# Letting GpSimd's jobs wait for the vector engine's last listed job on the shared SBUF port

## The chip, the cores and the metric

The kernel runs on one core of a Trainium2 chip. A core has five engines that work side by side, each through its own list of instructions, in order: TensorE (PE in the profile, with its weight loads as PEld), VectorE (DVE), ScalarE (ACT), GpSimd (POOL) and SyncE (SP), which here starts the transfers between HBM and SBUF. An instruction starts when those in front of it on its engine have been started and the semaphores that it names have reached their values. The metric is the time of one execution on the device, in microseconds (us); less is better.

## The reference

Attention with normalised queries and keys, and then two feed-forward layers, all in float32:

```python
def _attn_ref(q, k, v, g_q, g_k):           # batch 4, 12 heads, 448 rows, 64 columns
    q_n, k_n = (rmsnorm(q, g_q), rmsnorm(k, g_k))
    scores = q_n @ k_n.T / sqrt(64);  scores -= max(scores)
    attn = exp(scores);  attn /= sum(attn) + 1e-9
    return attn @ v

x = attention output as 1792 tokens x 768
h = x @ w_in;  x = (max(h, 0) ** 2) @ w_out                   # inner width 2048
g = x @ w_gate;  out = (g * sigmoid(g) * (x @ w_val)) @ w_out  # inner width 1536
```

## The kernel before

**Precision and tiles.** Products are made of float32 numbers split into a high and a low part: `hi` is a rounded copy, `lo = x - hi`, and a product is three matmuls (hi hi, hi lo, lo hi). So nearly every operand costs a copy (ACT or DVE, line 218 or 220 when it goes through `copy`) and a subtraction (DVE or POOL). Weights come as 64-bit words and are taken apart on DVE: lines 282 to 297 make the value from the two halves, 312 its low part. The attention goes over 24 pairs of heads; a pair has seven tiles of 128 rows. For each pair the kernel loads k and q (`kq`), squares them (`nat`, line 501 on POOL or 500 on ACT), sums the rows on DVE (506), finds the reciprocal root by three Newton steps (`rsqrt`: on DVE as one job for the first rows, else a begin on DVE, lines 448 and 449, and three jobs on POOL, lines 454 to 465, the last of which writes `stage`), lets PE transpose the result (`rows<-ident,stage`, 612), scales k (680, 683, or 595), splits k and q (`kst`, `kst_lo`, `qst`, `qst_lo`, 667), and then makes scores on PE (739), maxima on DVE (767, 768), exponentials on ACT (781), transposes on PE (845), their copies (218), the product with v (878), its scaling (900), and the split of the result into `x` (924 on POOL). The first part of the first feed-forward layer (`h_a`, `ya`) fills PE's gaps.

**The order of the work** is found while the program is built. The kernel is written as many small threads that yield jobs. A job names for each engine that may do it a planned time in ns; a planner with a clock of its own hands out the jobs, and in the order in which it hands them out the instructions are put on the engines' lists. That order is the list of work. On the chip each engine goes through its own list; between engines only the semaphores of the data hold.

The planner has a notion of a port that DVE and POOL share. A job's key `"G"` is POOL; `"W"` is DVE with operands in SBUF; `"V"` is DVE with an operand in PSUM, or a small one. A job on POOL and a `"W"` job on DVE are "ported": the planner starts one only when the last one's planned time is over.

```python
engines = {"P": nc.tensor, "A": nc.scalar, "V": nc.vector, "G": nc.gpsimd, "S": nc.sync}
def ported(job, e):
    return e == "G" or e == "V" and "W" in job[1][0]
...
if port[0] > clock[0]:
    q = [job for job in q if not ported(job, e)]
...
for e in engines:                     # who is asked, and in which order
    moved = dispatch(e) or moved
...
yield {"G": 900}, lambda e: step(e, ends if i == 2 else [(y, None)])      # rsqrt, three times
yield {"G": 1106, "W": 535}, lambda e: e.tensor_tensor(out=lo, in0=x, in1=as_f32(hi), op=ALU.subtract)
```

The exclusion is in the plan alone: in the program of before no semaphore stands for the port.

Of the kernel before, what the change touches and what calls it, by code (L numbers as in the profile page):

```python
# [78 lines left out]
def attention_two_ffn_kernel(  # L79
# [19 lines left out]
    nc = tc.nc  # L99
# [32 lines left out]
    engines = {"P": nc.tensor, "A": nc.scalar, "V": nc.vector, "G": nc.gpsimd, "S": nc.sync}  # L132
# [37 lines left out]
                heapq.heappush(timers, (clock[0] + p, serial[0], t, None))  # L170
            return

    port = [0.0]

    def meant(job):
        e = next(iter(job[1][0]))
        return "V" if e == "W" else e

    def cost(job, e):
        costs = job[1][0]  # L180
        return costs["W"] if e == "V" and "W" in costs else costs[e]

    def ported(job, e):
        return e == "G" or e == "V" and "W" in job[1][0]

    def late(job):

        e = meant(job)
        ahead = [o for o in queues[e] if not o[3] and (o[0].rank, o[2]) < (job[0].rank, job[2]) and meant(o) == e]
        return max(free_at[e] - clock[0], 0) + sum(cost(o, e) for o in ahead) + cost(job, e)  # L190

    def dispatch(e):
        queues[e] = [job for job in queues[e] if not job[3]]
        if not queues[e] or free_at[e] > clock[0]:
            return False
        q = [job for job in queues[e] if e == meant(job) or late(job) > cost(job, e) + spare[e]]
        if port[0] > clock[0]:
            q = [job for job in q if not ported(job, e)]
        if not q:
            return False  # L200
        job = min(q, key=lambda job: (job[0].rank, job[2]))
        job[3] = True
        t, p, _, _ = job
        p[1](engines[e])
        done = free_at[e] = clock[0] + cost(job, e)
        if ported(job, e):
            port[0] = done
        if e == "S":
            dma_free[0] = max(dma_free[0], clock[0] + 1100) + p[2] / DMA_RATE
            done = dma_free[0] + 900  # L210
        else:
            done += p[2] if len(p) > 2 else settle[e]
        heapq.heappush(timers, (done, job[2], t, e))
        return True
# [13 lines left out]
    def simulate(done):  # L228

        while not done():  # L230
            moved = True
            while moved:
                moved = False
                for entry in sorted(blocked, key=lambda entry: (entry[0].rank, entry[0].n)):
                    if entry[1]():
                        blocked.remove(entry)
                        resume(entry[0], None)
                        moved = True
                for e in engines:
                    moved = dispatch(e) or moved  # L240
            if done():
                return
            times = [timers[0][0]] if timers else []
            times += [free_at[e] for e in engines if queues[e] and free_at[e] > clock[0]]
            times += [port[0]] * (port[0] > clock[0])
            clock[0] = min(times)
            while timers and timers[0][0] <= clock[0]:
                _, _, t, value = heapq.heappop(timers)
                resume(t, value)
# [1063 lines left out]
```

## Time and profile before

| | |
|---|---|
| time of three runs | 1293.56, 1297.56, 1297.2 us; median 1297.2 |
| the profiled execution | 1290.19 us; its span, first to last instruction, 1288.4 us |
| busy in the span | PE 1258.1 us (98%), DVE 667.6 (52%), ACT 573.0 (44%), POOL 156.3 (12%) |
| granted TensorE clock | 0.999 of full speed in the mean |

The attention takes about the first 420 us; what follows is the two feed-forward layers. Names such as `kst_lo<-kq,kst` say what an instruction writes and reads. Busy PE time is modelled from pipelined matmuls.

### The profile page before, as it was taken

Reading aid. Unit: us, or ns where it says so; the run is one execution under the profiler, and the core shown is the slowest. Engines: PE = TensorE matmul, PEld = TensorE weight load, DVE = VectorE, ACT = ScalarE, POOL = GpSimd, SP = SyncE. Lnnn points to the kernel's source line nnn. Section 1 sums busy time; section 2 is a strip of 40 time slices with the busy share of each in tenths; the row PEclk is TensorE's granted clock in tenths of the full one; section 3 lists DMA queues with packets and bytes.
Section 4 is the critical chain, followed back from the end, with each engine's and each line's share of the span. In section 5 each row is a group of like instructions: output and inputs, shape, how many; then the busy total and the mean of one; then the engine's idle time right before and its main releaser. Section 6 shows DMA issues by size and latency. Waiting matters only on the chain.

```text
span 1288.4 us, 18441 instructions
## 1 busy us (share of the span) xinstructions
PE 1258.1 (98%) x6710; PEld 1079.9 (84%) x6710; DVE 667.6 (52%) x1357; ACT 573.0 (44%) x1257; POOL 156.3 (12%) x263
## 2 busy tenths in 40 slices
PE   8878999999999999999999999999999999999998
PEld 6555777777777999999999999999999999999998
DVE  7999964554543997249333783212148712213122
ACT  6898986776775656135322442212126411202110
POOL 4443633443210000000000000000000000000000
PEclk9999999999999999999999999999999999999999
DMA  6567564344313667137343563010127500203021
GB/s 210 150 200 197 161 189 124 110 123 134 93 43 104 209 192 254 52 114 226 113 129 129 172 206 126 21 65 7 37 63 232 154 1 1 86 1 129 1 86 43
DMA packets 85469, 151.02 MB, mean 117 GB/s; under 512 B 14641, under 2 KB 64962, under 8 KB 85378
## 3 DMA queue, kind: packets, MB, share of 16 engines
q1 hardware_dynamic: 85378, 149.84, 37.0%
q8 instruction: 53, 0.87, 0.3%
q14 instruction: 38, 0.31, 0.1%
HBM read 120.75 MB, written 29.04 MB: 116 GB/s over the span
## 4 chain that ended last, share of the span: by engine, by line
PE 83%; DVE 7%; ACT 4%; DMA 2%; issue 2%; POOL 1%; SPq 0%; DVEq 0%; ACTq 0%; POOLq 0%
PE y L325 27%; PE h_v L325 14%; PE h_g L325 14%; PE h L325 12%; PE ya L325 4%; PE o L878 3%; PE pt L845 3%; PE h_a L325 3%; PE sc L739 3%; DVE sc L767 2%; ACT ring L781 2%; ACT turned_p L218 1%; DVE ss L506 1%; DMA raw_out<-in_w_out_dram 1%; PE h_lead L325 1%
## 5 line engine op out<-in xcount | busy, mean ns | idle before, releaser
L325 PE MATMUL h_v<-x,hi_v 128*128 128x448 f32 x576 | 164.4, 366 | 0.0
L325 PE MATMUL h_g<-x,hi_g 128*128 128x448 f32 x576 | 164.3, 366 | 0.0
L325 PE MATMUL y<-s,hi_o 128*128 128x448 f32 x576 | 164.1, 366 | 0.0
L325 PE MATMUL y<-s,hi_out 128*128 128x448 f32 x552 | 157.2, 366 | 0.0
L325 PE MATMUL h<-x,hi_in 128*128 128x448 f32 x516 | 147.4, 367 | 0.0
L378 DVE TENSOR_TENSOR sig<-h_g,sig 128x448 f32<-128x448 f32 x48 | 29.9, 623 | 216.7 <-ACT sig L377 216.7
L781 ACT ACTIVATE ring<-sc,m,rms 128x448 f32<-128x448 f32 x168 | 124.0, 741 | 29.8 <-PE pt L845 20.2
L377 ACT ACTIVATE sig<-h_g 128x448 f32<-128x448 f32 x48 | 26.1, 544 | 219.3 <-PE h_g L325 219.2
L325 PEld LDWEIGHTS h_v<-x,hi_v 128*128 128x128 f32 x576 | 108.2, 188 | 9.3
L325 PEld LDWEIGHTS h_g<-x,hi_g 128*128 128x128 f32 x576 | 108.2, 188 | 9.2
L325 PEld LDWEIGHTS y<-s,hi_o 128*128 128x128 f32 x576 | 108.1, 188 | 9.3
L767 DVE TENSOR_REDUCE sc<-sc 128x2 f32<-128x896 f32 (+1 forms) x96 | 93.8, 977 | 38.0 <-PE sc L739 37.6
L325 PEld LDWEIGHTS y<-s,hi_out 128*128 128x128 f32 x552 | 103.5, 188 | 8.8
L845 PE MATMUL pt<-ident,ring 128*128 128x128 f32 x672 | 101.8, 276 | 9.2 <-ACT turned_p L218 2.9
L845 PEld LDWEIGHTS pt<-ident,ring 128*128 128x128 f32 x672 | 78.8, 140 | 33.5 <-ACT turned_p L218 6.6
L325 PE MATMUL h_v<-x,lo_v 128*128 128x448 f32 x288 | 105.4, 366 | 0.0
L325 PE MATMUL y<-s,lo_o 128*128 128x448 f32 x288 | 105.4, 366 | 0.0
L325 PE MATMUL h_g<-x,lo_g 128*128 128x448 f32 x288 | 105.4, 366 | 0.0
L325 PEld LDWEIGHTS h<-x,hi_in 128*128 128x128 f32 x516 | 96.9, 188 | 8.6
L218 ACT COPY turned_p<-pt 128x512 f32<-128x512 f32 x165 | 97.0, 596 | 11.0 <-PE pt L845 10.8
L325 PE MATMUL y<-s,lo_out 128*128 128x448 f32 x276 | 100.8, 365 | 0.0
L325 PE MATMUL h<-x,lo_in 128*128 128x448 f32 x258 | 94.5, 366 | 0.0
(155 smaller groups left out, 2135.8 us busy)
## 6 DMA issues: line engine op xcount, KB each, us to landing
raw_in<-in_w_in_dram SPq DMA_DIRECT2D x32, 384.0 KB, 3.3
raw_out<-in_w_out_dram SPq DMA_DIRECT2D x32, 384.0 KB, 3.5
kq<-in_kq_p_dram SPq DMA_DIRECT2D x23, 480.0 KB, 3.6
xr<-x2d SPq DMA_DIRECT2D x42, 224.0 KB, 4.8
raw_g<-in_w_gate_dram SPq DMA_DIRECT2D x24, 384.0 KB, 3.1
raw_v<-in_w_val_dram SPq DMA_DIRECT2D x24, 384.0 KB, 3.6
raw_o<-in_w_out_dram SPq DMA_DIRECT2D x24, 384.0 KB, 4.0
xr<-x1d SPq DMA_DIRECT2D x36, 224.0 KB, 4.5
```

Source lines behind the costliest of these rows:

```text
L218: e.copy(out, src)
L325: return {"P": 203}, lambda e: e.matmul(ps, lhsT=w, rhs=x, start=first, stop=last), 0
L377: yield {"A": 424}, lambda e: e.activation(out=t, in_=pg, func=ACTF.Sigmoid)
L378: yield {"V": 535}, lambda e: e.tensor_tensor(out=t, in0=pg, in1=t, op=ALU.mult)
L506: yield {"V": 535}, lambda e: e.tensor_reduce(out=stat["ss", b][:, w, p], in_=rows, axis=AX.X, op=ALU.add)
L739: e.matmul(parts[t][:, :S], lhsT=q[a][d, bass.ts(i % 4, 128)], rhs=k[c][d], start=(p == 0), stop=(p == len(passes) - 1),)
L767: e.tensor_reduce(out=top, in_=sc, axis=AX.X, op=ALU.max, negate=True)
L781: yield {"A": 704}, lambda e: e.activation(out=probs(at + t), in_=parts[t][:, :S], func=ACTF.Exp, bias=m[:, t:t + 1], scale=rq[:, i:i + 1] ...
L845: e.transpose(ps[:, bass.ts(j, 128)], p[:, bass.ds(min(128 * j, S - 128), 128)], ident)
L878: e.matmul(o[64 * h:64 * h + 64], lhsT=v[:, 4 * h + j], rhs=turned_p[:, 2 * j + h], start=(j == 0), stop=(j == 3),)
```

## The change

Each job on POOL now also waits, by a semaphore, for the end of the last ported job that the list of work has put on DVE ahead of it. Only the first instruction of the POOL job gets the wait. The reverse isn't added: a DVE job does not wait for POOL's jobs. The planned times and the planner's rules are not touched.

```diff
-    port = [0.0]
+    port, port_last = [0.0], []
+    behind = mybir.DependencyInfo(mybir.DependencyClass.Sync, mybir.DependencyReason.DATA)
+
+    def traced():
+        return nc.cur_bb.bb.instructions
 
     def meant(job):
...
         job[3] = True
         t, p, _, _ = job
+        before = len(traced())
         p[1](engines[e])
+        if ported(job, e):
+            if e == "V":
+                port_last[:] = [traced()[-1]]
+            elif port_last:
+                first = next(i for i in traced()[before:] if i.engine == engines["G"].engine)
+                tc.add_manual_dep(first, port_last[0].name, behind, reason="port")
         done = free_at[e] = clock[0] + cost(job, e)
```

## Rows read from the trace of the kernel before

**Rows 1.** Stretches: length, busy PE, PEld, DVE, ACT, POOL; clock, DMA share, GB/s.
```profile
16.00:165.00 149.00, 129.86 (x886) 87.66 (x884) 137.36 (x284) 129.12 (x314) 70.42 (x110) 0.99 0.62 182
165.00:420.00 255.00, 250.91 (x1506) 186.65 (x1507) 124.44 (x242) 178.44 (x423) 77.36 (x121) 1.00 0.38 113
420.00:1288.00 868.00, 864.67 (x4239) 795.29 (x4237) 395.02 (x792) 258.68 (x509) 3.51 (x3) 1.00 0.33 105
```
**Rows 2.** The chain that ended last, by line: 16 to 165 us, then 165 to 420.
```profile
by line: DVE sc L767 13.8%; ACT ring L781 8.3%; issue 8.3%; DMA raw_out<-in_w_out_dram 5.3%; ACT turned_p L218 4.3%; DMA raw_in<-in_w_in_dram 3.7%; DVE ss L506 3.4%; DVE wt_in L297 3.0%; DMA rkb<-rkd 2.7%; PE sc L739 2.3%; PE o L878 2.2%; D
...
by line: PE ya L325 19.7%; PE o L878 16.1%; PE pt L845 13.8%; PE h_a L325 13.1%; PE sc L739 12.2%; ACT ring L781 3.4%; issue 2.5%; ACT turned_p L218 2.5%; DMA raw_in<-in_w_in_dram 2.2%; DMA nat<-in_k_n_dram 1.9%; DVE sc L767 1.9%; PE rows L
```

**Rows 3.** Timeline of DVE and POOL from 115.90 us: start, duration in us.
```profile
115.90 0.68 DVE L680 SCALAR_TENSOR_TENSOR kq<-kq,gqk,rkb 128x448 f32<-128x448 f32 x1
...
116.49 0.55 DVE L294 SCALAR_TENSOR_TENSOR wt_out<-wa_out,wt_out 128x384 int32<-128x384 int32 x1
...
116.66 1.40 POOL L924 TENSOR_TENSOR x<-ox,x 128x448 fp32r<-128x448 f32 x1 [2.37 <-ACT x L218]
...
116.96 1.58 DVE L680 SCALAR_TENSOR_TENSOR kq<-kq,gqk,rkb 128x448 f32<-128x448 f32 x1
```

**Rows 4.** DVE's instructions by line, 16 to 165 us: ns least/median/most, first and last start.
```profile
L282 DVE TENSOR_SCALAR wa_in<-raw_in x1: 1424/1424/1424, 69.5 to 69.5; 128x384 f32<-128x384 f32 x1
...
L290 DVE TENSOR_SCALAR wt_in<-raw_in x12: 347/357/1110, 18.6 to 89.0; 128x384 int32<-128x384 uint32 x12
L290 DVE TENSOR_SCALAR wt_out<-raw_out x12: 345/354/1295, 97.5 to 158.4; 128x384 int32<-128x384 uint32 x12
...
L294 DVE SCALAR_TENSOR_TENSOR wt_out<-wa_out,wt_out x12: 544/559/1352, 97.9 to 160.8; 128x384 int32<-128x384 int32 x12
...
L297 DVE SCALAR_TENSOR_TENSOR wt_in<-wa_in,wt_in x12: 544/552/1436, 31.5 to 90.7; 128x384 int32<-128x384 int32 x12
L297 DVE SCALAR_TENSOR_TENSOR wt_out<-wa_out,wt_out x12: 505/548/1511, 101.5 to 165.0; 128x384 int32<-128x384 int32 x12
...
L220 DVE CAST kst<-kq x3: 379/471/1477, 69.2 to 123.0; 128x448 fp32r<-128x448 f32 x3
L220 DVE CAST qst<-kq x2: 415/890/1365, 39.9 to 68.8; 128x512 fp32r<-128x512 f32 x2
...
L463 DVE SCALAR_TENSOR_TENSOR rms<-rst,rms x3: 189/1027/1114, 57.1 to 59.3; 128x28 f32<-128x28 f32 x2, 128x14 f32<-128x14 f32 x1
...
L667 DVE TENSOR_TENSOR kst_lo<-kq,kst x2: 611/980/1349, 70.8 to 125.6; 128x448 fp32r<-128x448 f32 x2
...
L680 DVE SCALAR_TENSOR_TENSOR kq<-kq,gqk,rkb x2: 676/1130/1584, 115.9 to 117.0; 128x448 f32<-128x448 f32 x2
```

**Rows 5.** The same stretch grouped by shape: busy us, mean ns, idle us before.
```profile
L294 DVE SCALAR_TENSOR_TENSOR wt_out<-wa_out,wt_out 128x384 int32<-128x384 int32 x12 | 8.8, 743 | 0.1
```

**Rows 6.** Timeline of an rsqrt chain on POOL, from 175.89 us.
```profile
175.89 0.18 DVE L449 TENSOR_SCALAR rms<-ss 128x28 int32<-128x28 int32 x1
...
176.15 0.47 POOL L454 TENSOR_TENSOR rst<-rms 128x28 f32<-128x28 f32 x1 [4.35 <-DVE rms L449]
...
177.24 1.10 DVE L767 TENSOR_REDUCE sc<-sc 128x2 f32<-128x896 f32 x1
...
177.94 0.23 POOL L454 TENSOR_TENSOR rst<-rms 128x28 f32<-128x28 f32 x1
...
179.21 0.23 POOL L454 TENSOR_TENSOR rst<-rms 128x28 f32<-128x28 f32 x1
```

**Rows 7.** Instructions that write or read kst_lo, whole span; columns as in rows 4.
```profile
L739 PEld LDWEIGHTS sc<-kst_lo,qst x161: 183/186/192, 23.3 to 389.4; 64*128 64x128 f32 x138, 128*128 128x128 f32 x23
...
L667 POOL TENSOR_TENSOR kst_lo<-kq,kst x21: 1131/1149/1467, 19.6 to 361.6; 128x448 fp32r<-128x448 f32 x21
```

**Rows 8.** Idle time (us, times) before stage's and before L506's instructions, by releaser.
```profile
  POOL stage L465: 5.7, 7
...
  POOL nat L501: 6.9, 6
```

## The prediction

> **What bounds the kernel now.** I read the busy time by stretch first [rows 1]. TensorE (PE) is idle for 149 - 129.86 = 19.1 us from 16 to 165 us, 255 - 250.91 = 4.1 us from 165 to 420, and 868 - 864.67 = 3.3 us in all the time after that. GpSimd (POOL) has 110 and 121 instructions in the first two of these stretches and three in the last. So the change can only act before 420 us, and a gain has to come above all out of the 19.1 us. In that stretch the vector engine (DVE) is busy 137.36 of 149 us, ScalarE (ACT) 129.12, POOL 70.42. Next I read the chain in the same two stretches [rows 2]: from 16 to 165 it runs through DVE's reductions and ACT's exponentials, with single PE lines at 2%; from 165 on it is PE's own matmuls (19.7%, 16.1%, 13.8%, 13.1%, 12.2%). So a microsecond of DVE's is worth something before 165 us and next to nothing behind it.
>
> Then I looked at what POOL and DVE do to each other [rows 3]. POOL's job x starts at 116.66, while DVE's L294 runs to 116.49 + 0.55 = 117.04. POOL's job takes 1.40 us and ends at 118.06. DVE's L680, which came to its start at 116.96, takes 1.58 us, though the same instruction had taken 0.68 just before; it ends at 118.54, half a microsecond after x. The two engines exclude each other already, in the order in which they arrive. DVE's reductions are not part of it: the one at 177.24 takes 1.10 us, and a POOL step that starts under it at 177.94 takes its 0.23 us [rows 6].
>
> **The change part by part.**
>
> *What it removes: DVE's time behind POOL.* The longest instruction of each of DVE's groups between 16 and 165 us against the usual one of its group [rows 4]: L290 1.110 - 0.357 = 0.75 and 1.295 - 0.354 = 0.94; L282, of the same shape, 1.424 - 0.357 = 1.07; L297 1.436 - 0.552 = 0.88 and 1.511 - 0.548 = 0.96; the casts at L220 1.477 - 0.471 = 1.01 and 1.365 - 0.415 = 0.95; L463 1.027 - 0.189 = 0.84 and 1.114 - 0.189 = 0.93; L667 1.349 - 0.611 = 0.74; L680 1.584 - 0.676 = 0.91. L294 has more than one long member, so by its mean [rows 5]: 12 x (743 - 559 ns) = 2.2. Sum 12.2 us. All of these are jobs that the planner counts as users of the pair ("W").
>
> The bounds of the gain: zero, if in each of these meetings DVE's job is listed behind POOL's (then there is no new wait); 12.2 us, if in each it is listed ahead, so that POOL stands back and DVE runs on. Which it is no row shows. The kernel gives a lean: when the pair comes free, the planner asks DVE before POOL, so of two jobs that both wait DVE's is listed first. Against it: POOL runs later than planned in the rsqrt chains (a step is planned at 900 ns; the first instructions of two successive steps stand at 177.94 and 179.21, 1.27 us apart [rows 6]), and a POOL job that is late comes behind its DVE job without any new wait. I take half: 6.1 us.
>
> How much of DVE's time reaches the end: in the chain from 16 to 165 us the three DVE lines that the row shows have 13.8 + 3.4 + 3.0 = 20% [rows 2], the lower bound. The upper one is DVE's busy share there, 137.36 of 149 us or 92% [rows 1], if DVE set the pace throughout. ACT's two lines and three transfers have another 8.3 + 4.3 + 5.3 + 3.7 + 2.7 = 24% of the chain, which DVE's time can't shorten, so I stay below the middle: 40%, or 6.1 x 0.4 = 2.4 us gained. From 165 to 420 us, where the chain is PE's, I count nothing.
>
> The trace shows the waiting of rows 3 as whole instructions, not as slower ones. The Trainium skill, "SBUF — State Buffer", section "Who interferes with whom", says the same: whoever issues first gets the shared port pair for the whole instruction, and the other fully blocks. By that rule alone the change only swaps who stands still, and the sum would hold 0 in place of 2.4 us.
>
> *What it adds: waits on POOL's side.* A POOL job that starts today while its DVE job runs waits for the pair anyway; a semaphore in its place costs the release, 0.08 us from the end of L449 (175.89 + 0.18) to the POOL step at 176.15 [rows 6]. The dearer case is a POOL job that starts today before its listed DVE job has begun: it then waits for the queue in front of that job as well, one reduction of 1.10 us and a weight job of 0.55 us, 1.65 us together [rows 4, 6]. Behind a waiting POOL instruction stand POOL's next jobs, in order. Who waits for those:
> PE's scores need kst_lo and qst_lo. POOL's first kst_lo starts at 19.6 us, takes 1.47 us at most, and is first loaded at 23.3 [rows 7]: 2.2 us of cover, more than the 1.65. Where the cover is gone, each microsecond of POOL's is one of PE's.
> DVE's row sums (L506) waited for POOL's squares six times, 6.9 us in all [rows 8]. A later square can add its delay there; DVE has 11.6 us idle in the stretch in any case [rows 1], and I count 0.
> PE's transposes of the rsqrt rows waited for POOL's last step (stage) in 7 of 10 chains, 5.7 us in all [rows 8]. There a delay of POOL is a delay of PE, one for one. Each chain has three POOL jobs, so 30 new waits. The first step of a chain follows a DVE job anyway (L449). For the twenty later ones the bounds are 0 and 20 x (0.55 + 0.08) = 12.6 us, with a weight job of DVE's put between all steps. The chain that I read lies near the lower bound: its second step starts under a reduction, and the first instructions of both later steps take 0.23 us, where the first step's took 0.47 behind a weight job [rows 6]. I take 1 us.
>
> Sum: 2.4 - 1.0 = 1.4 us faster. The profiled execution, 1288.4 us of span and 1290.19 us in all, would become 1288.8 us. It lies 7 us under the median of the runs shown, 1297.2 us; the same step from that median gives 1295.8 us.
>
> A measurement of this kernel tells about 0.3%, 3.9 us, from no change.
>
> **The rivals.**
> *Forecast: a small exchange* (DVE gets a few microseconds back, PE gets a late transpose here and there): 1295.8 us, own range 1293 to 1298. Chance 0.45.
> *The order holds* (faster): most of the meetings of rows 4 have DVE's job listed first, and DVE's next job is a reduction, under which POOL runs free. Then 10 to 12.2 us of DVE come back in the stretch where it is the chain, and 60 to 90% reach the end: 6 to 11 us, so 1286 to 1291. For it: the planner asks DVE first, and 13.8 + 3.4 of the 20% that DVE's rows have in the chain are reductions (L767, L506 [rows 2]). Against it: transfers of weights have 9% of the chain already (raw_out and raw_in [rows 2]) and take more of it once DVE is quicker. Chance 0.29.
> *The chains come late* (slower): the planner asks DVE first between two rsqrt steps too, so a weight job is listed there, and each later step now waits for it. At 0.63 us a wait, one in each of the 7 chains for which PE stood waiting is 4.4 us, two are 8.8 us. It decides once more than about half of the later steps have a DVE job in front that is not done. Then 1300 to 1304, with part of DVE's gain taken off. For it: PE waits at this very place [rows 8]. Against it: the chain of rows 6. Chance 0.18.
> *Nothing happens*: nearly every listed job is done when POOL comes, or POOL, released at the end of one DVE job, meets the next one already holding the pair, so that the same meetings stand one job later: 1297.2 us. Chance 0.08. The rule of the skill quoted above ends here.
>
> **How the numbers follow.** Within 0.3% are the last rival and the forecast but for a small tail: 0.08 + 0.41 = 0.49. Faster: 0.29 + 0.04 = 0.33. Slower: 0.18. For the range I leave out the best tenth (all 12.2 us would give 1285.0) and the worst tenth (both later steps late in every chain): 1287 to 1302.
>
> **What would show it.** In the profile after: the long DVE instructions of rows 4 fewer, DVE's busy time from 16 to 165 us lower by 3 to 9 us; POOL waiting with DVE's weight lines (L290, L294, L297, L312, L366) as releaser, where the step of today names L449; POOL's own long durations (the 1.40) back at about 1.15, which is 1.149 for the usual kst_lo [rows 7]; PE's 19.1 us smaller by about what the whole gains. For the late chains: more than 5.7 us of waiting for stage, and rsqrt steps further apart than 1.27 us with L294 or L297 as releaser. The forecast is wrong if new waits pile up in one place, as POOL's squares behind a weight job that itself waits for its transfer, or if DVE's gain reaches the end in full.

## The result, and the profile after

| | median us | range us | runs |
|---|---|---|---|
| before | 1294.73 | 1292.89 to 1297.56 | 5 |
| with the change | 1285.24 | 1280.69 to 1287.19 | 5 |

The ratio is 0.9919, with a 95% interval of 0.9892 to 0.9946: faster by 0.8%, some 10.5 us. The profiled execution took 1280.69 us with a span of 1278.9 us, 9.5 us less than that of before. The median of before, from five runs here, is 2.5 us lower than that of the three runs that the prediction started from. The kernel's lines from 218 on have numbers 11 higher than before (L297 is now L308). Ratios leave out executions more than 1.5% above the fastest of the same kernel: one of e9's twelve and three of e15's, below.

Busy time by stretch, after (columns as in [rows 1]):

```profile
16.00:165.00 149.00, 135.96 (x936) 92.77 (x937) 137.04 (x296) 136.27 (x331) 69.27 (x112) 1.00 0.67 196
165.00:420.00 255.00, 252.06 (x1502) 189.08 (x1502) 124.44 (x244) 176.12 (x416) 74.70 (x119) 1.00 0.37 111
```

In the same 149 us PE does 936 matmuls in place of 886, and its idle time falls from 19.1 to 13.0 us. DVE is as busy as before, but with 296 instructions in place of 284: its time went into work. The same piece of DVE's list can be followed in both traces. Its reductions that stand at 42.9, 60.4, 74.3, 119.9 and 177.2 us before come 1.1, 3.8, 5.3, 7.0 and 9.3 us earlier after; from 180 us to 430 us the distance stays within 8.9 and 9.5. All of the gain is made before 180 us.

The place of [rows 3], after: timeline of DVE and POOL.

```profile
110.78 0.67 DVE L691 SCALAR_TENSOR_TENSOR kq<-kq,gqk,rkb 128x448 f32<-128x448 f32 x1
111.37 0.55 DVE L305 SCALAR_TENSOR_TENSOR wt_out<-wa_out,wt_out 128x384 int32<-128x384 int32 x1
111.84 0.68 DVE L691 SCALAR_TENSOR_TENSOR kq<-kq,gqk,rkb 128x448 f32<-128x448 f32 x1
112.43 0.55 DVE L308 SCALAR_TENSOR_TENSOR wt_out<-wa_out,wt_out 128x384 int32<-128x384 int32 x1
112.90 1.09 DVE L778 TENSOR_REDUCE sc<-sc 128x2 f32<-128x896 f32 x1
113.12 1.14 POOL L935 TENSOR_TENSOR x<-ox,x 128x448 fp32r<-128x448 f32 x1 [3.82 <-DVE wt_out L308]
...
114.10 1.10 DVE L778 TENSOR_REDUCE sc<-sc 128x2 f32<-128x896 f32 x1
114.22 1.15 POOL L678 TENSOR_TENSOR kst_lo<-kq,kst 128x448 fp32r<-128x448 f32 x1
```

This is the mechanism in eight lines. POOL's x is listed behind DVE's weight job L308 (L297 before), and now waits for its end. DVE runs its four jobs in a row, none of them stretched (L691 takes 0.68 us where it took 1.58), and reaches its reduction at 112.90. Only then does POOL start, and x and kst_lo run in 1.14 and 1.15 us under two reductions that take their usual 1.09 and 1.10. Before, the two POOL jobs and two DVE jobs had stood in each other's way for almost two microseconds; the second pair, which [rows 3] breaks off at, was this:

```profile
118.10 1.47 POOL L667 TENSOR_TENSOR kst_lo<-kq,kst 128x448 fp32r<-128x448 f32 x1
118.47 1.51 DVE L297 SCALAR_TENSOR_TENSOR wt_out<-wa_out,wt_out 128x384 int32<-128x384 int32 x1
```

DVE's instructions by line from 16 to 165 us, after (columns as in [rows 4], where the same groups stand):

```profile
L293 DVE TENSOR_SCALAR wa_in<-raw_in x1: 348/348/348, 65.7 to 65.7; 128x384 f32<-128x384 f32 x1
...
L301 DVE TENSOR_SCALAR wt_in<-raw_in x13: 345/354/1068, 18.4 to 158.0; 128x384 int32<-128x384 uint32 x13
L301 DVE TENSOR_SCALAR wt_out<-raw_out x12: 344/352/1297, 92.4 to 150.2; 128x384 int32<-128x384 uint32 x12
...
L305 DVE SCALAR_TENSOR_TENSOR wt_out<-wa_out,wt_out x12: 543/548/1425, 92.8 to 151.9; 128x384 int32<-128x384 int32 x12
...
L308 DVE SCALAR_TENSOR_TENSOR wt_in<-wa_in,wt_in x13: 545/550/564, 30.3 to 160.1; 128x384 int32<-128x384 int32 x13
...
L231 DVE CAST qst<-kq x2: 415/883/1351, 37.9 to 65.0; 128x512 fp32r<-128x512 f32 x2
...
L474 DVE SCALAR_TENSOR_TENSOR rms<-rst,rms x3: 168/188/192, 55.0 to 56.4; 128x28 f32<-128x28 f32 x2, 128x14 f32<-128x14 f32 x1
...
L678 DVE TENSOR_TENSOR kst_lo<-kq,kst x2: 612/614/617, 66.0 to 116.8; 128x448 fp32r<-128x448 f32 x2
...
L691 DVE SCALAR_TENSOR_TENSOR kq<-kq,gqk,rkb x4: 673/679/685, 110.8 to 164.1; 128x448 f32<-128x448 f32 x4
```

The long members of L293, L308 (wt_in), L474, L678 and L691 are gone; L301, L305 and one cast keep theirs. New long ones have come, as at L459 (0.94 us at 120.02) and here, behind an x that had waited for ScalarE:

```profile
40.29 1.14 POOL L935 TENSOR_TENSOR x<-ox,x 128x448 fp32r<-128x448 f32 x1 [1.30 <-ACT turned_p L229]
40.38 1.46 DVE L323 TENSOR_TENSOR lo_in<-wt_in,hi_in 128x384 fp32r<-128x384 f32 x1
```

To compare runs I add up, for the DVE instructions between 16 and 165 us that overlap a POOL instruction and take over 0.25 us more than is usual for their form, what they take too long. Before it is 14.0 us on 17 instructions (the prediction's 12.2 us, L312's 0.3, a third long L297's 0.3, L800's 0.9 and roundings), after 6.5 us: 7.5 us less. This sum is called DVE's lost time below.

Who POOL waited for from 16 to 165 us, after (us in all, times, longest):

```profile
POOL x L935 <- DVE wt_out L308: 3.8, 1, 3.8
...
POOL nat L512 <- DVE hi_out L231: 3.4, 1, 3.4
POOL rst L465 <- DVE wt_in L305: 2.5, 1, 2.5
POOL rst L465 <- DVE lo_out L323: 2.5, 1, 2.5
POOL kst_lo L678 <- DVE wt_in L308: 2.3, 1, 2.3
```

These releasers are new. Counted in the two programs, 57 of POOL's instructions name a DVE semaphore, against 26 before; for most jobs the wait adds no new name, because an earlier wait of POOL's covers it or one on DVE was there and only its value rises. The wait for the chains, whole span (idle us, times, as in [rows 8]):

```profile
  POOL stage L476: 6.8, 10
```

### The profile page after: what moved, and what is told of

The parts are those of the page before. It is cut to its first block, busy times and chain, and to the rows that moved or that the text cites. A ratio compares the mean times of both kernels' runs of the same rounds, so it can differ in the third digit from the quotient of the medians.

```text
span 1278.9 us, 18467 instructions
## 1 busy us (share of the span) xinstructions
PE 1256.5 (98%) x6710; PEld 1079.3 (84%) x6710; DVE 660.1 (52%) x1357; ACT 572.7 (45%) x1257; POOL 152.1 (12%) x263
## 4 chain that ended last, share of the span: by engine, by line
PE 84%; DVE 6%; ACT 4%; DMA 3%; POOL 1%; issue 1%; SPq 0%; ACTq 0%; DVEq 0%; POOLq 0%
PE y L336 27%; PE h_v L336 14%; PE h_g L336 14%; PE h L336 12%; PE ya L336 4%; PE o L889 3%; PE pt L856 3%; PE sc L750 3%; PE h_a L336 3%; ACT ring L792 2%; DVE sc L778 1%; ACT turned_p L229 1%; DMA zb<-zd 1%; DVE ss L517 1%; DMA raw_in<-in_w_in_dram 1%
```

## The experiments

Every ratio is to the kernel before, run beside it on the same chip. What a run costs against the change is the difference of the two ratios times 1294 us, and as uncertain as both.

**Which waits: early or late, nine or the rest.** The job's number in POOL's list decides whether it gets the wait:

```diff
+        nth[0] += e == "G"
...
-            elif port_last:
+            elif nth[0] < 61 and port_last:       # e1;  e2: nth[0] >= 61
+            elif nth[0] in {1, 19, 20, 22, 23, 39, 40, 41, 42} and port_last:   # e3;  e4: not in
```

*e1, the first 61 jobs.* 

> The new wait only on POOL's first 61 jobs in the list (those that stand before about 166 us in the profile of before); the other 73 jobs wait as before. Theory A (DVE is the pace of the first 165 us, and what the wait gives back of its time is what the whole gains): all of the gain, ratio to the kernel before 0.990 to 0.994. Theory B (the gain is of many small effects along the whole attention, POOL being held to the plan everywhere): about half, 0.995 to 0.997.

*e2, the other 73.* 

> The new wait only on the 73 jobs behind the first 61. Theory A: PE's own work is the chain there, so nothing, ratio 0.998 to 1.002. Theory B: the other half of the gain, 0.995 to 0.997.

*e3, nine jobs.* 

> The new wait only on nine of POOL's jobs: the squares at 18.5, 70.7 and 124.2 us of the profile of before, kst_lo at 57.6 and 118.1, kq at 59.3, qst_lo at 69.4 and 122.9, x at 116.7. They are the ones that stood in front of DVE instructions that are short in the profile after. Theory A: 0.8 + 1.8 + 1.5 + 3.3 = some 7.4 us of the 9.5 us of span, ratio 0.993 to 0.995. Theory B: nine waits of 134 give next to nothing, 0.998 to 1.001.

*e4, all but these nine.* 

> The new wait on all of POOL's jobs but those nine. Theory A: what is left, some 2 us, ratio 0.997 to 0.9995. Theory B: nearly all of the gain, 0.992 to 0.994.

| | ratio (interval) | DVE's lost time, 16 to 165 us |
|---|---|---|
| before | 1 | 14.0 us |
| the change | 0.9919 (0.9892 to 0.9946) | 6.5 |
| e1 | 0.9920 (0.9902 to 0.9938) | 5.7 |
| e2 | 1.0003 (0.9992 to 1.0015) | 14.7 |
| e3 | 0.9941 (0.9923 to 0.9959) | 6.5 |
| e4 | 0.9970 (0.9959 to 0.9981) | 13.0 |

The waits before 166 us carry the whole gain and those behind it nothing, as theory A had it. Nine waits of 134 carry 7.6 us (0.0059 x 1294), for 7.5 us of DVE's lost time. The rest of the waits give 3.9 us with only 1.0 us of lost time less; that is at the edge of what theory A allowed (0.997), and theory B's "nearly all" is further off.

**Does order help as such, or who stands back?** *e7, the wait the other way round.*

```diff
-            if e == "V":
+            if e == "G":
...
-                first = next(i for i in traced()[before:] if i.engine == engines["G"].engine)
+                first = next(i for i in traced()[before:] if i.engine == engines["V"].engine)
```

> The wait the other way round and alone: DVE's jobs on SBUF operands wait for the last POOL job listed ahead of them, POOL's wait for nothing new. Theory A (the gain comes from sparing DVE): no gain, 0 to 4 us slower than the kernel before, ratio 0.999 to 1.004. Theory C (keeping to the planned order is what helps, whichever engine stands back): a gain like that of the change, 0.991 to 0.996.

Measured: 1300.80 us, ratio 1.0052 (1.0037 to 1.0068), 6.7 us slower than before, more than theory A's 4. Who DVE waited for from 16 to 165 us in this kernel:

```profile
DVE wt_in L305 <- POOL rms L476: 1.2, 1, 1.2
...
DVE wt_out L305 <- POOL rms L476: 1.1, 1, 1.1
DVE wt_out L308 <- POOL rms L476: 1.0, 1, 1.0
DVE wt_in L308 <- POOL kst_lo L678: 1.0, 1, 1.0
DVE lo_out L323 <- POOL rms L476: 0.9, 1, 0.9
```

The same planned order, enforced from the other side, makes DVE stand idle for POOL's chains. So the order as such brings nothing; it matters that DVE is the engine that is let through.

**Do the waits in the chains cost?** *e8, no new wait for the rsqrt jobs.*

```diff
-            elif port_last:
+            elif port_last and p[0] != {"G": 900}:
```

> The change, but the three rsqrt jobs of a chain on POOL get no new wait. By the prediction's term for late chains (1 us lost): 1 us faster than the change, ratio 0.990 to 0.992. If the waits in the chains spare DVE as well: 0 to 1 us slower than the change, ratio 0.992 to 0.993. No difference clear of noise is a possible answer.

Measured: ratio 0.9925 (0.9906 to 0.9944), not to be told from the change. Neither the loss that the prediction counted for the chains nor a gain is seen; with some 4 us of uncertainty either way, a loss of 1 us could not have been.

**What DVE's time is worth.** Work is put on DVE that nothing needs. *e5 and e6, eight reductions done twice* (the second writes the same values):

```diff
-                e.tensor_reduce(out=top, in_=sc, axis=AX.X, op=ALU.max, negate=True)
+                for _ in range(2 if g in range(2, 10) and 4 in tiles else 1):    # e6: range(13, 21)
+                    e.tensor_reduce(out=top, in_=sc, axis=AX.X, op=ALU.max, negate=True)
```

> The changed kernel, and for the head pairs 2 to 9 one of DVE's score reductions is done twice (the second time it writes the same values): eight more instructions of about 1.09 us on DVE, 8.7 us, in the first 165 us. Theory A (DVE sets the pace there, a microsecond of DVE is a microsecond of the whole): nearly all of the gain is lost again, ratio to the kernel before 0.996 to 0.999. The share of 0.4 that the prediction took: 3.5 us, ratio 0.994 to 0.996.

> The same eight doubled reductions, but for the head pairs 13 to 20, where the chain is TensorE's. Theory A: little, 0 to 2 us of the 8.7, ratio to the kernel before 0.991 to 0.994. If DVE's time costs the same everywhere: 0.996 to 0.999.

Measured: e5 0.9960 (0.9945 to 0.9975), e6 0.9950 (0.9930 to 0.9969): 5.3 and 4.0 us of the 8.7. Both lie between the answers that were to be told apart, and the intervals overlap. Not decisive.

*e9, nine useless reductions exactly where DVE had stood behind POOL, and e10, nine elsewhere.* The keys are places in DVE's list:

```diff
+    spent = const.tile([128, 6], F32, name="spent")
...
+        if e == "V":
+            for _ in range({48: 1, 118: 2, 149: 1, 150: 1, 240: 1, 241: 1, 248: 1, 249: 1}.get(on_v[0], 0)):
+                nc.vector.tensor_reduce(out=spent, in_=ident.unsqueeze(1).to_broadcast([128, 6, 128]), ...)
...
# e10: [71, 101, 136, 160, 186, 211, 223, 266, 280]
```

> The changed kernel, and in front of the nine DVE jobs that stood behind POOL in the kernel before (at 18.6, 57.7, 59.3, 69.5, 70.8, 117.0, 118.5, 123.1 and 124.4 us of its profile) a useless reduction of about 0.9 us on DVE that writes to a tile nobody reads: the lost time is put back at its places, without POOL. Theory A (at these places DVE's time is the whole's time, one for one): 0.9 x 9 = some 8 us of the gain are lost, ratio to the kernel before 0.997 to 1.000. The share of 0.4 that the prediction took: 3.2 us, ratio 0.994 to 0.996.

> The changed kernel with the same nine useless reductions in front of nine other weight jobs of DVE's between 31 and 140 us, away from the places where it stood behind POOL. If DVE's time is worth the same throughout that stretch: as with the reductions at the places themselves, ratio 0.997 to 1.000. If the places matter (elsewhere DVE has slack in front of ScalarE or of a transfer): 0.993 to 0.996.

Measured: e9 0.9972 (0.9941 to 1.0003), an interval that is wide because its twelve runs spread from 1283.8 to 1304.9 us; e10 0.9932 (0.9908 to 0.9955). By themselves these ratios would say that DVE's time is worth little. But the traces show a second effect. In e9 DVE's list is 8.5 us behind the changed kernel's at 165 us, as expected for 8.5 us of reductions, and 9.1 us at 500 us; from there it catches up evenly and ends 3.5 us behind. Nothing of the edit lies in those 800 us except that the new tile of 24 bytes on each partition may have moved others. So the run was repeated without a new tile, and the tile was tried alone.

*e13, the nine reductions without a new tile* (they write into the tile of gains, g, which is no longer read):

```diff
-                nc.vector.tensor_reduce(out=spent, in_=ident.unsqueeze(1).to_broadcast([128, 6, 128]), ...)
+                nc.vector.tensor_reduce(out=g_at[0][:, 0:1], in_=ident.unsqueeze(1).to_broadcast([128, 6, 128]), axis=AX.XY, ...)
```

> As the run with nine useless reductions of about 0.95 us at the places where DVE stood behind POOL, but they write into a tile that exists already and is no longer read, so that no tile is moved. Theory A (DVE's time at these places is the whole's time): 8.5 us of the gain lost, ratio to the kernel before 0.998 to 1.001, and the last 800 us as long as in the changed kernel. With the share of 0.4: 0.994 to 0.996.

Measured: 1293.23 us, ratio 0.9994 (0.9981 to 1.0006); span 1288.8 us, that of before within half a microsecond. The reductions in this kernel, and the place of [rows 3] once more:

```profile
L210 DVE TENSOR_REDUCE g<-ident x9: 902/947/958, 18.6 to 124.2; 128x1 f32<-128x768 f32 x9
```

```profile
117.13 0.95 DVE L210 TENSOR_REDUCE g<-ident 128x1 f32<-128x768 f32 x1
118.00 0.68 DVE L697 SCALAR_TENSOR_TENSOR kq<-kq,gqk,rkb 128x448 f32<-128x448 f32 x1
118.59 0.94 DVE L210 TENSOR_REDUCE g<-ident 128x1 f32<-128x768 f32 x1
119.45 0.55 DVE L314 SCALAR_TENSOR_TENSOR wt_out<-wa_out,wt_out 128x384 int32<-128x384 int32 x1
119.92 1.09 DVE L784 TENSOR_REDUCE sc<-sc 128x2 f32<-128x896 f32 x1
120.14 1.13 POOL L941 TENSOR_TENSOR x<-ox,x 128x448 fp32r<-128x448 f32 x1 [5.24 <-DVE wt_out L314]
```

All of the new waits are in this kernel, POOL runs under the reductions as in the changed one, and yet the gain is gone: 9 x 0.947 = 8.5 us of DVE's time, put where POOL had taken it, cost 0.0075 x 1294 = 9.7 us (6 to 14 by the intervals). The score reduction stands at 119.92 us, where it stood at 119.90 before. This is theory A's answer, and the share of 0.4 is out.

*e16, nine such reductions between 193 and 356 us.* 

> The changed kernel with nine useless reductions of about 0.95 us on DVE, without a new tile, in front of nine DVE jobs between 200 and 365 us, where the chain is TensorE's. If DVE's time is worth nothing there, as the prediction counted: ratio as the change, 0.990 to 0.994. If it costs 0.4 of itself, as the doubled reductions behind 200 us did: 3.4 us, 0.993 to 0.996.

Measured: 0.9940 (0.9923 to 0.9957), 2.7 us of the 8.5; by the intervals anything from nothing to 7 us. In the trace the list is 0.3 us behind the changed kernel's at 180 us, 3.2 at 300 and 3.1 at the end. So the trace puts DVE's time behind 165 us at about a third; the ratio alone would allow nothing.

**A tile that moves the others.** *e14 and e15, the tile alone, with and without the change.*

```diff
+    spent = const.tile([128, 6], F32, name="spent")
+    nc.vector.memset(spent, 0.0)
```

> The changed kernel with one more constant tile of 24 bytes on each partition, which is set once and never read, and no reductions. If the tile moves the others and that is what shortened the last stretch: 4 to 6 us faster than the change, ratio to the kernel before 0.986 to 0.990. If the shorter stretch came from elsewhere: as the change, 0.990 to 0.994.

> The kernel before with that tile alone, without the new wait. If the tile's effect is real and independent of the wait: 4 to 6 us faster than the kernel before, ratio 0.995 to 0.997. Else 0.999 to 1.001.

Measured: e14 1277.76 us, ratio 0.9881 (0.9861 to 0.9902). This is the lowest median of all, though the interval still touches the change's. e15: ratio 0.9978 (0.9945 to 1.0012), median 1289.20 beside 1293.64 of before; its twelve runs spread from 1285.4 to 1306.1, which makes the interval wide. Busy time from 500 to 900 us, first the changed kernel, then e14:

```profile
500.00:900.00 400.00, 400.00 (x1964) 368.41 (x1963) 180.04 (x352) 121.50 (x236) 2.05 (x2) 1.00 0.36 117
```

```profile
500.00:900.00 400.00, 400.00 (x1976) 370.66 (x1975) 182.47 (x357) 125.69 (x246) 2.05 (x2) 1.00 0.37 120
```

PE has no gap in either, at the same granted clock, and does twelve matmuls more in 400 us with the tile.

Up to 500 us a list's place in one trace against another tells less: e14's, without any reduction, is 4.7 us behind the changed kernel's there, and e6's is 5.4 us behind at 200 us, ahead of its first added reduction at 211.4. (The trace of the changed kernel is of the fastest of its five executions.) So the 8.5 and 9.1 us read from e9 are not all its reductions. The ratios say more. Against e14, which has the tile too, e9's nine reductions cost 11.8 us (0.0091 x 1294; 7 to 17 by the intervals) and e10's 6.6 (3 to 11). The first is theory A's answer once more; whether the places matter stays open. The price of DVE's time rests on e3, on e13, and on e9 against e14.

**A better plan.** *e11 and e12, the rsqrt step planned at 1270 ns, with and without the wait.*

```diff
-            yield {"G": 900}, lambda e: step(e, ends if i == 2 else [(y, None)])
+            yield {"G": 1270}, lambda e: step(e, ends if i == 2 else [(y, None)])
```

> The changed kernel, with the planner's cost of an rsqrt step on POOL set from 900 to the 1270 ns that the profile shows, so that the list of work expects POOL where it really is. Theory A: the stretched DVE instructions that the change leaves before 165 us (6.5 us in all, most of them behind POOL jobs that follow a chain) become fewer, and the whole gains up to 4 us more, ratio 0.987 to 0.991. The order of the list changes too, which can bring a few us either way: 0.987 to 0.997 is possible.

> The kernel before, without the new wait, with the same planner's cost of 1270 ns for an rsqrt step. Theory A: a better plan alone spares DVE less than the wait does, since POOL still starts ahead of DVE jobs that are late: ratio 0.995 to 1.001. If the plan's error in the chains were the whole cause, it would bring what the change brings, 0.989 to 0.994.

Measured: e11 0.9966 (0.9954 to 0.9978), e12 1.0001 (0.9989 to 1.0013). The truer cost alone changes nothing, as expected. With the wait it is 6 us slower than the change (2 to 10 by the intervals); with the new cost the planner lists the attention in another order (DVE's list differs from its 68th instruction on), and these runs don't tell the cost's effect from the new order's. DVE's lost time, added up as above, is 6.6 us in e12 and 3.3 in e11. So e12 loses as little as the change and gains nothing: the sum compares only kernels with the same list. Between e11 and e12, whose lists are the same, it holds again: the wait takes 3.3 us off the lost time and gains 4.5 us (0.0035 x 1294).

## Why the prediction was wrong

*What bounds the kernel: right.* The gain arose before 180 us, by e1 and e2 from the waits of that part alone.

*Exclusion in order of arrival, whole instructions: right,* and half-right in its use. The sentence of the Trainium skill, "SBUF — State Buffer", section "Who interferes with whom", agrees with both traces, but the sum of 0 that it would give when each stall only changes sides did not come. The side that now stands back is POOL, and it starts under reductions, which take 1.09 and 1.10 us with POOL beside them and without. The same section of the Trainium skill says that a tensor_reduce on trn2 never contends for the pair; the trace agrees with that too.

*How much of DVE's lost time comes back: right in size,* in part by luck. Half of 12.2 us was taken, 6.1 us; 7.5 of 14.0 us came back. The half is a balance: most of the old meetings went, and new ones came (L323, L459), which the prediction had not thought of. What remains stands mostly behind POOL jobs that are listed ahead of DVE's and are late; the prediction had named the lateness of the rsqrt chains (150.25 us in the changed kernel, L301, 1.30 us, behind a kst_lo that follows a chain), but x is late for ScalarE too. DVE's busy time did not fall by the 3 to 9 us that were to show the gain: later work moved up into the same 149 us.

*The share of it that reaches the end: this step failed.* The prediction took 0.4, between the part of the chain that DVE's lines hold (20%) and DVE's busy share (92%). The runs show about 1, and the prediction had named this, DVE's gain reaching the end in full, as a sign that it is wrong. e3: 7.5 us of lost time less, 7.6 us gained. e13: 8.5 us of DVE put back, 9.7 us lost. The change itself: 7.5 us less, 10.5 us by the ratio. By their intervals e3 gained at least 5.3 us and e13 lost at least some 6, where 0.4 would give 3.0 and 3.4. e5 alone, with 5.3 of 8.7 us, lies lower, and its interval holds both answers. The explanation is this: an engine with 137.36 busy us of 149 [rows 1], whose list is in order and has no other place to catch up, passes each delay on. The mistake was to read the chain's shares as prices: the chain names ACT's exponentials or a weight transfer (raw_out) at a moment, but an exponential starts behind DVE's maxima, and a weight transfer needs a tile that DVE's L290 has set free. That these links carried the delay is read from the kernel; no run cut them one by one. The busy share was the better estimate.

*Nothing behind 165 us: wrong in size, without effect here.* e16's trace gives a third. It didn't matter, because the waits behind 166 us spare DVE almost nothing (e2).

*The chains, 1 us lost: not found.* The wait for stage did rise from 5.7 to 6.8 us, by about what was counted, but e8, without these waits, is not measurably faster; 1 us is less than that comparison tells.

*The rivals.* "The order holds" came nearest, with 6 to 11 us, but not by its own terms: 7.5 us came back, where it had 10 to 12.2, and about all of that reached the end, where it had 60 to 90%. That the product fits is luck. What spoke against it, that transfers of weights would take the chain over, did not stop it: raw_in and raw_out hold 6.1% and 3.4% of the chain there afterwards, 9.5% against 9%:

```profile
by line: ACT ring L792 11.4%; DVE sc L778 8.4%; ACT turned_p L229 6.1%; DMA raw_in<-in_w_in_dram 6.1%; issue 5.6%; DMA zb<-zd 4.8%; DMA nat<-in_q_n_dram 4.0%; DVE ss L517 3.5%; DMA raw_out<-in_w_out_dram 3.4%; PE pt L856 2.3%; DVE wt_in L30
```

"The chains come late" has its mirror in e7, where POOL's chains do hold up DVE, and it costs 6.7 us.

With a share of 1 and without the loss in the chains the prediction's own terms give 6.1 us. The rest of the distance to 1285.24 us is 1.4 us of lost time that it put too low, 2.5 us of the starting median, and some 2 to 3 us that DVE's lost time doesn't account for, in the change (9.5 by the medians and 10.5 by the ratio, against 7.5) as in e4 (3.9 against 1.0). The intervals are 3 us wide on either side. The granted clock of TensorE goes with this rest. In the runs of the experiments the executions of before had a clock of 0.994 of full speed in the mean, and so had those of e2 and e12, which gain nothing; the change and e4 had 0.997, e1 0.998, e3 0.996, e13 0.995. A straight line through before's own executions gives 0.5 to 1.1 us less for each thousandth more, which makes three thousandths an estimated 1.5 to 3.5 us. The profiles show such a stretch, first before, then after (columns as in [rows 1]):

```profile
36.00:43.50 7.50, 4.82 (x36) 3.71 (x38) 7.40 (x14) 6.23 (x16) 6.67 (x16) 1.00 0.69 192
43.60:47.00 3.40, 3.40 (x25) 2.41 (x25) 3.33 (x8) 2.73 (x9) 0.34 (x1) 0.50 0.66 212
```

```profile
36.00:43.50 7.50, 5.78 (x52) 4.11 (x50) 7.36 (x15) 6.83 (x17) 4.99 (x13) 1.00 0.69 221
43.60:47.00 3.40, 3.40 (x27) 1.54 (x27) 3.37 (x8) 3.35 (x11) 0.61 (x1) 1.00 0.50 128
```

Before, PE stands idle for 2.7 of 7.5 us, and then the clock is at its lower level, 1.2 GHz, for 3.4 us; after, PE is idle for 1.7 us there, and the clock stays at 2.4 GHz. The trace of e4 has one such stretch, as that of before has, and between these two the span differs by 1.4 us (1287.0 against 1288.4) for 1.0 us of lost time. So the clock may well be the rest, and a part of the share of about 1 in e3 and e13 too; no run changed the clock alone, so this is not shown.

## What to carry to other kernels

Where two engines exclude each other on a port, ask which of them is the pace, and let the other one wait by a semaphore until the first reaches work that doesn't need the port: nine such waits were worth 7.6 us, and the wait turned round, on all of DVE's jobs, cost 6.7. Price an engine's lost time by how busy its in-order list is in that stretch, not by its share of the chain (here 92% and a price of about 1), and only between kernels with the same list. And if the price is in doubt, put useless work of a known length at the very place, without moving a tile, and look at the granted clock of every run.

## What the runs showed of the hardware that was not expected

A constant tile of 24 bytes on each partition that nobody reads made the last 800 us of the kernel some 5.5 us shorter (5.4 to 6.1 in the four traces), at a granted clock of 1.00 and with PE busy throughout: 1976 in place of 1964 matmuls in 400 us. All four kernels that had it (e9, e10, e14, e15) did 1975 or 1976 there, and all the others 1963 or 1964. The only link seen is that the tile can move the ones allocated after it; which of them matters, and to whom, was not tried. The runs of e9 and e15 spread over 21 us, those of e14 over 5.5; that isn't explained either.
